# A retention and MLP kernel: seven products in the first MLP product from block 4 instead of 6, and a third of the v scalings on GpSimd

## The chip, the cores and the metric

The kernel runs on one core of a Trainium2 chip. TensorE (PE) multiplies matrices into PSUM, VectorE (DVE) and ScalarE (ACT) read PSUM and SBUF, GpSimd (POOL) works on SBUF and issues loads, SyncE (SP) issues transposing DMAs and stores. The metric is device time in microseconds, as the median of several runs; less is better.

## The reference

Inputs are q, k, v of shape (8, 8, 576, 64) and the weights `w_in` (512 x 2048) and `w_out` (2048 x 512), all float32. The output is (4608, 512) in float32.

```
scores = q @ k^T / sqrt(64)                       # per batch and head
D[i, j] = gamma_h ** (i - j) for i >= j, else 0   # gamma_h = 1 - 2 ** (-5 - h)
x = (scores * D) @ v, heads side by side          # 4608 tokens x 512
out = gelu_exact(x @ w_in) @ w_out
```

## The kernel before

Attention runs in 36 units of 128 tokens; four units make a block of 512 tokens, so there are nine blocks, 0 to 8. For a unit, TensorE forms the scores (L516, L525 or L535), VectorE applies the mask (`masked`, L558), TensorE multiplies with v (`inner`, L600) and adds what earlier tokens left in the state `u` (`cross`, L653), and VectorE moves the result into the tile `x` (`evacuate`, L672). The state itself is a product of k with v scaled by a decay (`state`, L619). That scaled v is the tile `vh`, made in `scaled_v`: eight small ScalarE instructions, one a head (L572), for the units in the set `BY_ACT`, else one VectorE instruction (L575).

Then each block passes an MLP. The first product, x times `w_in`, with gelu on the way out of PSUM into the tile `g`, has two forms. The plain one (`mlp1`, L701) takes 64 matmuls of 512 columns for a block. The other (`fast`, L966) is a Strassen-like scheme: in each of four groups it forms seven products of half-size blocks instead of eight, P1 to P7, with four matmuls of 256 columns each, 112 for a block. It needs sums of weights (`sum_in`, `sum_last`), sums of x (`sum_x`, L939), and copies and adds between PSUM banks, through a scratch tile `p`, between its steps (L981, L985 and L461). `FAST = 6` and `ALL_FAST = 6` say that blocks 6, 7 and 8 take it.

The second product, g times `w_out`, also has seven products (M1 to M7, `part`, L885) in all blocks but block 0 (`mlp2`, L746). Three sums of g for each group (`sum_g`, L782 to L786) and sums of w_out (`sum_w`) feed it; `after` moves and combines its results into the output tiles, which `store` sends out.

No scheduler of the compiler orders this. The kernel runs a planner while it is built: the table `T` holds a due time for each engine, `on` adds a cost to it, and the loop at the end picks what TensorE does next by ready times (`mlp_pick`, `part_ready`, `fast_ready`, `may_begin`). First and second products of neighbouring blocks are interleaved, and attention groups are put between them. `either` gives a copy to VectorE or ScalarE, whichever would end it first. The string `ORDER` lists the loads in the order in which GpSimd issues them, followed by tokens that shift single decisions: `a28` puts unit 28's v on ScalarE, `s4+1.5` delays scores, `p32+28` holds back a group of the first product, and so on. Each engine works through its own list in order; semaphores hold it back where data or a buffer is missing. Loads wait in GpSimd's queue like any other instruction. `warm` fills gaps before 16 us of the plan with matmuls on zeros.

Of the kernel before, what the change touches and what calls it, by code (L numbers as in the profile page):

```python
# [9 lines left out]
FP32 = mybir.dt.float32  # L10
BF16 = mybir.dt.bfloat16
# [6 lines left out]
def kernel(  # L18
# [52 lines left out]
    FAST, ALL_FAST = 6, 6  # L71
    N_LD = 5
    N_QKT = 4
# [6 lines left out]
    HOLD = 9  # L80

# [6 lines left out]
    g_pool = ctx.enter_context(tc.tile_pool(name="g", bufs=1))  # L88
# [53 lines left out]
    def constants():  # L142
# [7 lines left out]
        far_at = on("dve", 0.55, at)  # L150
        nc.vector.tensor_scalar(ident, val, 0.0, None, op0=ALU.is_equal)
        on("dve", 0.35)
# [6 lines left out]

    N_NEAR, NEAR = 5, (0, 2, 4, 6, 1, 3, 5, 7)  # L160
# [27 lines left out]
    def sum_w(i):  # L188
        w = w_out_sb[i]
        s = w_sum[i] = const.tile([128, 5, 256], BF16, name=f"w_sum{i}")  # L190
        b11, b12, b21, b22 = w[:, 0, 0:256], w[:, 0, 256:512], w[:, 1, 0:256], w[:, 1, 256:512]
        nc.vector.tensor_tensor(s[:, 0], b11, b22, op=ALU.add)
        nc.vector.tensor_tensor(s[:, 1], b12, b22, op=MINUS)
        nc.vector.tensor_tensor(s[:, 2], b21, b11, op=MINUS)
        nc.vector.tensor_tensor(s[:, 3:5], w[:, :, 0:256], w[:, :, 256:512], op=ALU.add)
        ws_at[i] = on("dve", 1.05, land_out[i]) + SEM

# [87 lines left out]
    def load(what, i):  # L285
# [8 lines left out]
        if what == "dq":  # L294
# [6 lines left out]
            dq_at[i] = on("pool", 1.2, dq_at[i - 1])  # L301
# [23 lines left out]
    for x, keys in enumerate(zip(*HW_FIRST)):  # L325
        for n, (what, i) in enumerate(keys):
# [3 lines left out]
    ORDER = ("wi1 k1 wi0 io q1 v0 q2 k2 v1 wi2 v2 k3 wi3 q3 v3 wi4 wi5 wi6 k4 q5 k5 q4 v5 wi7 wo1 wo0 k6 v4 dq2 "  # L330
# [7 lines left out]
             "b21+6.0").split()  # L338

    BY_ACT = {int(x[1:]) for x in ORDER if x[0] == "a"}  # L340
    S_LATE = {int(x[1:].split("+")[0]): float(x.split("+")[1]) for x in ORDER if x[0] == "s"}
    B_LATE = {int(x[1:].split("+")[0]): float(x.split("+")[1]) for x in ORDER if x[0] == "b"}
    DVE_LAG, P_WAIT, HURRY = ({int(x[1:].split("+")[0]): float(x.split("+")[1]) for x in ORDER if x[0] == kind} for kind in "zpu")
    ORDER = [x for x in ORDER if x[0] not in "abszpu"]
# [76 lines left out]
    DRAIN = 0.25  # L421
    SEM = 0.12
# [140 lines left out]
    def scaled_v(i):  # L563
# [5 lines left out]
        by_act = i in BY_ACT  # L569
        if by_act:  # L570
            for h in range(H):
                nc.scalar.activation(vh[:, h, :], loaded[i][1][:, h, :], AF.Copy, scale=dv[:, h, ci:ci + 1])  # L572
            st[i]["V"] = on("act", 2.0, at) + SEM
        else:
            nc.vector.tensor_tensor(vh, loaded[i][1], dv[:, :, ci:ci + 1].to_broadcast([128, H, D]), op=ALU.mult)  # L575
            st[i]["V"] = on("dve", 0.685, at) + SEM
# [109 lines left out]
    def g_of(t, mm):  # L686
        return g_tiles[t, mm // 2][:, mm % 2] if t else g_tiles[t, mm // 2][mm % 2]

    def g_done(t, j):
        if t > 0 and all((t, 4 * j + x, ts) in g_at for x in range(4) for ts in range(4)):  # L690
            at = max(g_at[t, 4 * j + x, ts] for x in range(4) for ts in range(4)) - SEM
            for x in range(3):
                queued.append((at, x, sum_g, (t, j, x)))
# [654 lines left out]
```

## Time and profile before

| | |
|---|---|
| median of 3 runs | 285.56 us (285.5 to 286.11) |
| span of the profiled execution | 283.7 us |
| TensorE busy | 278.0 us, 98% |
| VectorE busy | 199.7 us, 70% |
| ScalarE busy | 158.8 us, 56% |
| GpSimd busy | 114.0 us, 40% |
| mean granted TensorE clock | 0.998 |

The span reaches from the first to the last instruction of one execution; for that execution the page gives no time of its own beside it, so the median of the runs stands for it, 1.86 us more. Busy time of an engine counts its compute instructions; GpSimd's also counts the issuing of its loads. In the rows, "x60" is the number of instructions, then come busy time and the mean duration of one in ns, then the idle time before them with what ended it. In the timeline the first number is the start and the second the duration, in us.

### The profile page before, as it was taken

The page shows a single profiled execution, that of the slowest core. Times are in us where ns is not written, and L with a number is a line of the kernel's source. Part 1 is how long each engine was busy: PE and PEld are TensorE (multiplying, and loading weights), DVE is VectorE, ACT ScalarE, POOL GpSimd, SP SyncE. Part 2 cuts the span into 40 slices and gives each one's busy share as a digit, 9 for nine tenths or more (in the row PEclk, how much of TensorE's full clock was granted, in tenths as well). Part 3 has the DMA queues.
Part 4 walks back from the last instruction along what each step waited for, and adds up shares of the span by engine and source line. Part 5 has one row for each costly group of instructions (what it writes and reads, how often), then busy time and mean ns, then how long its engine had stood idle before and what let it go on. Part 6 is the DMA issues. An engine that isn't in the chain of part 4 may idle for free.

```text
span 283.7 us, 8075 instructions
## 1 busy us (share of the span) xinstructions
PE 278.0 (98%) x3361; PEld 207.6 (73%) x3361; DVE 199.7 (70%) x412; ACT 158.8 (56%) x362; POOL 114.0 (40%) x143
## 2 busy tenths in 40 slices
PE   8989999999999999999999999999999999999994
PEld 3577666688874588548855778558888888888894
DVE  5753483979865595898178867889669968966822
ACT  5676724755456635693298874564565374665320
POOL 8979987993364465625468552000000000000000
PEclk9999999999999999999999999999999999999999
DMA  9999999999999999999999999910003000400133
GB/s 150 165 182 173 188 180 163 146 142 147 172 161 195 190 147 128 156 229 149 135 197 203 147 137 150 222 21 2 0 2 128 23 2 0 151 0 2 74 114 111
DMA packets 152804, 35.39 MB, mean 125 GB/s; under 512 B 141120, under 2 KB 148928, under 8 KB 152768
## 3 DMA queue, kind: packets, MB, share of 16 engines
q0 software_dynamic: 116832, 18.10, 95.3%
q1 hardware_dynamic: 34528, 16.26, 32.9%
q10 hardware_dynamic: 1408, 0.52, 0.7%
q8 instruction: 26, 0.43, 0.7%
q14 instruction: 10, 0.08, 0.1%
HBM read 36.70 MB, written 9.44 MB: 163 GB/s over the span
## 4 chain that ended last, share of the span: by engine, by line
PE 92%; POOL 3%; DMA 3%; issue 0%; DVE 0%; POOLq 0%
PE m L885 35%; PE hT L701 29%; PE f L966 13%; PE oT L746 5%; PE o_ps L600 3%; PE sc L535 3%; DMA w_in<-in_moe_w_in_dram 3%; POOL qk L318 2%; PE o_ps L653 1%; PE u_ps L619 1%; PE qk_ps L482 1%; POOL v_ld L318 1%; POOL w_in L291 1%; PE sc L525 0%; PE o_ps L591 0%
## 5 line engine op out<-in xcount | busy, mean ns | idle before, releaser
L701 PE MATMUL hT<-xT,w_in 128*128 128x512 bf16 (+3 forms) x560 | 87.4, 312 | 0.8 <-DMA w_in<-in_moe_w_in_dram 0.8
L710 ACT ACTIVATE g<-hT 128x512 bf16<-128x512 f32 (+2 forms) x106 | 57.7, 556 | 36.9 <-PE hT L701 36.1
L701 PEld LDWEIGHTS <-w_in 128*128 128x128 bf16 x560 | 48.4, 98 | 33.8 <-DMA w_in<-in_moe_w_in_dram 1.0
L885 PEld LDWEIGHTS <-gs 128*128 128x128 bf16 x656 | 62.2, 98 | 7.7
L885 PE MATMUL m<-w_sum,gs 128*128 128x256 bf16 (+1 forms) x400 | 47.7, 268 | 0.0
L318 POOL DMA_DIRECT2D v_ld<-in_v_dram x40 | 34.0, 854 | 19.3 <-DMA qk_ld<-in_k_dram 8.8
L318 POOL DMA_DIRECT2D qk_ld<-in_k_dram x36 | 30.4, 851 | 21.7 <-DMA qk_ld<-in_q_dram 19.1
L558 DVE TENSOR_TENSOR ret<-sc,msk 128x512 bf16<-128x512 f32 x48 | 30.2, 683 | 12.2 <-PE sc L535 12.2
L318 POOL DMA_DIRECT2D qk_ld<-in_q_dram x36 | 30.4, 851 | 16.9 <-DMA qkT<-qk_ld 6.5
L885 PE MATMUL m<-w_out,gs 128*128 128x256 bf16 x256 | 32.5, 273 | 0.0
L885 PE MATMUL m<-w_sum,g 128*128 128x256 bf16 x256 | 30.9, 273 | 0.0
L572 ACT ACTIVATE vh<-v_ld,dv 128x64 bf16<-128x64 bf16 x120 | 30.0, 339 | 0.0
L782 DVE TENSOR_TENSOR gs<-g 128x1024 bf16<-128x1024 bf16 x32 | 21.8, 686 | 9.0 <-ACT g L710 8.2
L885 PEld LDWEIGHTS <-g 128*128 128x128 bf16 x256 | 24.9, 98 | 3.9
L991 ACT ACTIVATE g<-f 128x512 bf16<-128x512 f32 x36 | 20.2, 590 | 8.9 <-PE f L966 7.5
L786 DVE TENSOR_TENSOR gs<-g 128x1024 bf16<-128x1024 bf16 x32 | 21.6, 684 | 0.0
L672 DVE TENSOR_TENSOR xT<-o_ps,dqT 128x512 bf16<-128x512 f32 (+1 forms) x32 | 18.4, 617 | 4.5 <-PE o_ps L653 4.4
L966 PEld LDWEIGHTS <-w_in 128*128 128x128 bf16 x192 | 18.8, 98 | 2.2
L461 ACT CAST u_sb<-u_ps 128x512 bf16<-128x512 f32 x15 | 8.7, 587 | 16.0 <-PE u_ps L619 16.0
L461 ACT COPY o<-m 128x512 f32<-128x512 f32 x14 | 8.2, 587 | 15.7 <-PE m L885 15.7
L987 ACT ACTIVATE g<-p 128x512 bf16<-128x512 f32 x12 | 7.6, 630 | 14.1 <-DVE p L985 14.1
L966 PEld LDWEIGHTS <-wi 128*128 128x128 bf16 x144 | 14.0, 98 | 1.6
(96 smaller groups left out, 337.6 us busy)
## 6 DMA issues: line engine op xcount, KB each, us to landing
out_dram<-o SPq DMA_DIRECT2D x27, 256.0 KB, 6.3
v_ld<-in_v_dram POOLq DMA_DIRECT2D x32, 128.0 KB, 9.1
qk_ld<-in_k_dram POOLq DMA_DIRECT2D x28, 128.0 KB, 10.7
qk_ld<-in_q_dram POOLq DMA_DIRECT2D x28, 128.0 KB, 8.6
w_in<-in_moe_w_in_dram POOLq DMA_DIRECT2D x8, 256.0 KB, 7.3
w_out<-in_moe_w_out_dram POOLq DMA_DIRECT2D x8, 256.0 KB, 8.0
out_dram<-o SPq DMA_DIRECT2D x14, 128.0 KB, 2.1
qk_ld<-in_q_dram POOLq DMA_DIRECT2D x8, 64.0 KB, 11.4
```

Of the source, the lines that this page charges most:

```text
L318: nc.gpsimd.dma_start(dst, src[2 * bp + jj, :, ci * C:ci * C + n, :].rearrange("h s d -> s h d"))
L461: nc.scalar.copy(dst, src)
L558: nc.vector.tensor_tensor(r, t, by, op=ALU.mult)
L572: nc.scalar.activation(vh[:, h, :], loaded[i][1][:, h, :], AF.Copy, scale=dv[:, h, ci:ci + 1])
L672: nc.vector.tensor_tensor(x_of(i)[:, :, n * x:n * x + n], o, dqT[:, :, ci * C:ci * C + n], op=ALU.mult)
L701: nc.tensor.matmul(hT[:, m, :], lhsT=w[:, cc, o:o + 128], rhs=x_tiles[t][:, cc, lo:hi], start=(cc == 0), stop=(cc == N_DM - 1))
L710: nc.scalar.activation(g_of(t, m0 // 2)[:, m0 % 2:m0 % 2 + n, lo:hi], hT, AF.Gelu)
L782: nc.vector.tensor_tensor(s.rearrange("p m a b -> p m (a b)"), g[:, :, 0, :], g[:, :, 1, :], op=ALU.add)
L786: nc.vector.tensor_tensor(s, g[:, :, :, LEFT], g[:, :, :, RIGHT], op=MINUS)
L885: nc.tensor.matmul(m[:, 0 if apart else ts, :], lhsT=a, rhs=w[:, c0:c1], start=p in begins and mm == 0 and ts == 0, stop=mm == N_DF // 2 - ...
L966: nc.tensor.matmul(m[:, y, :], lhsT=a[:, c], rhs=d[:, c], start=p in (P1, P7) and y == 0 and c == 0, stop=c == 1, skip_group_check=True)
L991: nc.scalar.activation(g[:, :, rows, cols], m, AF.Gelu)
```

## The change

The first product takes its seven-product form from block 4 on, so in blocks 4 to 8. The tile `g` of a block is cut in two halves that turn through three buffers, and the scratch tile `p` goes: its place is the part of `g` that is written last. Thirteen of the 36 v scalings move to GpSimd (tokens `g23` and the like in `ORDER`), four stay on ScalarE (fifteen before), nineteen on VectorE (21 before). The seven products of the second product are replaced by another set of seven, Q1 to Q7, which takes four sums of half the tile in place of three, each over two groups at once, except in the last block; its results are added in the output tile. The planner's costs are changed in places, it reckons with GpSimd and VectorE hindering each other, and the string `ORDER` is another one, with other loads from `wi4` on and other shifts. The diff, cut to its core:

```diff
-    FAST, ALL_FAST = 6, 6
+    FAST, ALL_FAST = 4, 4
     N_LD = 5
+    N_G = 3
...
-    g_pool = ctx.enter_context(tc.tile_pool(name="g", bufs=1))
+    g_pool = ctx.enter_context(tc.tile_pool(name="g", bufs=N_G))
...
-    def on(engine, dur, ready=0.0):
+    def on(engine, dur, ready=0.0, pair=False):
         lap = 0.075 if engine == "dve" and dur > 0.2 else 0.0
-        T[engine] = max(T[engine], ready) + dur - lap
+        start = max(T[engine], ready)
+        if pair:
+            for a, b in port[-2:]:
+                if a < start + dur and start < b:
+                    start = max(start, b - 0.1)
+            pairs_read.append((start, start + dur))
+        elif engine == "pool" and dur > 0.6:
+            for a, b in pairs_read[-4:]:
+                if a < start + dur and start < b:
+                    T["dve"] = max(T["dve"], min(start + dur + 0.5, T["dve"] + 1.5))
+            port.append((start, start + dur))
+        T[engine] = start + dur - lap
...
-    ORDER = ("wi1 k1 wi0 io q1 v0 q2 k2 v1 wi2 v2 k3 wi3 q3 v3 wi4 wi5 wi6 k4 q5 k5 q4 v5 wi7 wo1 wo0 k6 v4 dq2 "
+    ORDER = ("wi1 k1 wi0 io q1 v0 q2 k2 v1 wi2 v2 k3 wi3 q3 v3 wi4 q4 wi5 wi6 wo1 k4 q5 k5 dq2 v4 wo0 wi7 q6 v5 "
...
-        if by_act:
+        if i in BY_POOL:
+            nc.gpsimd.tensor_tensor(vh, loaded[i][1], dv[:, :, ci:ci + 1].to_broadcast([128, H, D]), op=ALU.mult)
+            st[i]["V"] = on("pool", POOL_V, at) + SEM
+        elif i in BY_ACT:
...
+        g_tiles[t, j // 2] = g_pool.tile([128, 4, 2, TOK], BF16, tag="g", name="g")
...
-    bank_of = {M3: "X", M4: "Y", M5: "X", M1: "Z", M2: "Y", M6: "V", M7: "Z"}
-    begins = {M3, M4}
-    behind = {M5: M3, M1: M4, M2: M4, M6: M1, M7: M1}
+    bank_of = {Q1: "X", Q6: "X", Q5: "X", Q3: "X", Q7: "V", Q4: "V", Q2: "Y"}
+    begins = {Q1, Q7}
+    behind = {Q6: Q1, Q2: Q1, Q4: Q7, Q5: "C21", Q3: "C22"}
...
-        if n == 0:
-            nc.vector.tensor_tensor(s.rearrange("p m a b -> p m (a b)"), g[:, :, 0, :], g[:, :, 1, :], op=ALU.add)
-        elif n == 1:
-            nc.vector.tensor_tensor(s[:, :, 0], g[:, :, 0, LEFT], g[:, :, 1, RIGHT], op=ALU.add)
-        else:
-            nc.vector.tensor_tensor(s, g[:, :, :, LEFT], g[:, :, :, RIGHT], op=MINUS)
+        o, a, b, op = {S1: (s1, a21, a22, ALU.add), S2: (s2, s1, a11, MINUS), S3: (s3, a11, a21, MINUS), S4: (s4, a12, s2, MINUS)}[n]
+        nc.vector.tensor_tensor(o, a, b, op=op)
...
+        nc.vector.tensor_tensor(hi[:, xs, d + c0:d + c1], m, hi[:, xs, d + c0:d + c1], op=ALU.add)
...
-            if not p7_tiles:
-                p7_tiles.append(ld_pool.tile([128, 2, 2, 256], FP32, tag="qk", bufs=N_LD, name="p7"))
-            f_bank[key, "p7"] = p7_tiles[0][:, j % 2]
+            f_bank[key, "p7"] = g.rearrange("p m a b -> p m (a b)")[:, :, 256:768].bitcast(FP32)
...
+    SEQ = (Q1, Q7, Q6, Q4, Q5, Q3)
+    FILL = ((Q5, (0, 1, 2, 3)),)
...
-            runs.append([("3", t, p, k) for p in range(7) for k in range(4)])
+            order = [(p, k) for p in SEQ for k in range(4) if p != Q2]
+            for at, ks in FILL if t < N_BLK - 1 else ((Q5, range(4)),):
+                n = order.index((at, 0)) if at is not None else len(order)
+                order[n:n] = [(Q2, k) for k in ks]
+            runs.append([("3", t, p, k) for p, k in order])
```

More of the change, by code (lines that the diff above doesn't have):

```diff
@@ new lines, in add_out @@
+    def add_out(t, n, what, done, ready):
+        hi = o_tiles[t, 1]
+        last = t == N_BLK - 1
+        b, m = held_bank[t, "X", n]
+        xs, c0, c1 = pieces(t)[n]
+        d = 256 * (what == "C22")
+        nc.vector.tensor_tensor(hi[:, xs, d + c0:d + c1], m, hi[:, xs, d + c0:d + c1], op=ALU.add)
+        seen(t, what, n, on("dve", 0.15 + 0.00104 * (xs.stop - xs.start) * (c1 - c0), max(done, ready)))
+        if last and n != 1:
+            x = xs.start
+            store(t, 2 + x, hi[:, x, d:d + 256], d, d + 256, *((nc.scalar, nc.scalar) if n else ()))
+        elif what == "C22" and not last:
+            for x in range(2):
+                store(t, 2 + x, hi[:, x, :])
```

308 lines of the change are left out of this document (177 added, 131 removed), and 15 rows, old and new, of the table ORDER.

## The prediction

> **What bounds the kernel now.** I read the page's head first, then the waits of TensorE, then its timeline.
>
> ```profile
> span 283.7 us, 8075 instructions
> PE 278.0 (98%) x3361; PEld 207.6 (73%) x3361; DVE 199.7 (70%) x412; ACT 158.8 (56%) x362; POOL 114.0 (40%) x143
> PE 92%; POOL 3%; DMA 3%; issue 0%; DVE 0%; POOLq 0%
> PE warm L1187 <- DVE zeros L118: 1.2, 1, 1.2
> PE hT L701 <- DMA w_in<-in_moe_w_in_dram: 0.8, 1, 0.8
> ```
>
> TensorE is busy for 98% of the span, and the chain that ended last runs through it for 92%. The two waits are all that the view of waits lists for its matmuls: 1.2 us before the first warm-up matmul and 0.8 us for a weight load. No wait for VectorE or ScalarE appears after that. So the span is the number of matmuls times their spacing, and a change is worth what it does to that product, as long as no new wait appears.
>
> The profiled span is 283.7 us and the median of the runs 285.56 us; the 1.86 us between them lie outside the span, and I keep them. The sum below is a difference, added to 285.56 us.
>
> **The price of one matmul.** A matmul's own duration (379 ns for 512 columns) includes the pipeline, so I take spacings from starts in the timeline of TensorE.
>
> ```profile
> 68.05 3.66 PE L885 MATMUL m<-w_sum,g 128*128 128x256 bf16 x32
> 71.54 1.91 PE L885 MATMUL m<-w_out,gs 128*128 128x256 bf16 x16
> 73.38 0.32 PE L591 MATMUL o_ps<-ret,vh 64*64 64x64 bf16 x16
> 73.53 0.30 PE L653 MATMUL o_ps<-qkT,u_sb 64*64 64x64 bf16 x16
> 73.76 0.61 PE L885 MATMUL m<-w_sum,gs 128*128 128x256 bf16 x4
> 80.29 0.64 PE L600 MATMUL o_ps<-ret,vh 128*64 128x128 bf16 x16
> ...
> 81.90 1.49 PE L885 MATMUL m<-w_sum,gs 128*128 128x256 bf16 x12
> 83.22 13.11 PE L701 MATMUL hT<-xT,w_in 128*128 128x512 bf16 x60
> 96.27 0.64 PE L600 MATMUL o_ps<-ret,vh 128*64 128x128 bf16 x16
> 217.31 0.60 PE L966 MATMUL f<-xT,wi 128*128 128x256 bf16 x4
> 217.84 0.64 PE L600 MATMUL o_ps<-ret,vh 128*64 128x128 bf16 x16
> ```
>
> With 256 columns: 71.54 - 68.05 = 3.49 us for 32, 0.109 us each. Four take 0.436 us, but 217.84 - 217.31 is 0.53: going from whole-array matmuls to the tiled ones of the attention costs 0.09 us. Sixteen 64x64 matmuls take 0.15 us (73.38 to 73.53) when the same tiling follows, and 0.23 us (73.53 to 73.76) when whole-array ones follow: the way back costs 0.08 us. With 512 columns: 96.27 - 83.22 = 13.05, less the 0.09 of the switch, by 60: 0.216 us. One group of the attention, 80 tiled matmuls, takes 81.90 - 80.29 = 1.6 us with its way back.
>
> **The change, part by part: TensorE.** Blocks 4 and 5 leave the plain first product. Each loses 64 matmuls of 512 columns (L701: 264 before, 136 in the built program after, 128 fewer for two blocks) and gets 112 of 256 columns.
>
> ```profile
> L701 PE MATMUL hT<-xT,w_in 128*128 128x512 bf16 x264 | 59.0, 379 | 0.0
> L966 PE MATMUL f<-xs,w_in 128*128 128x256 bf16 x96 | 14.4, 273 | 0.0
> L885 PE MATMUL m<-w_sum,gs 128*128 128x256 bf16 x368 | 46.7, 273 | 0.0
> ```
>
> That is -128 x 0.216 = -27.6 us and +224 x 0.109 = +24.4 us: -3.2 us. The second product keeps its seven products in other sums: 880 matmuls of 256 and 32 of 128 columns become 864 and 64, the same columns, and 16 more starts, some 0.1 us with the eight 384-column matmuls of block 0 that are cut into 24 of 128. Counted in the built programs, TensorE goes into tiled stretches 37 times where it went 31 times, and switches between tilings 13 times where it did 16: 6 x (0.09 + 0.08) - 3 x 0.09 = +0.75 us. Two more warm-up matmuls of 512 columns stand before the attention: +0.43 us if they fill no wait, nothing if they do; I take the whole. TensorE: -3.2 + 0.1 + 0.75 + 0.43 = -1.9 us.
>
> **VectorE and ScalarE.** Durations, one row for each kind:
>
> ```profile
> L558 DVE TENSOR_TENSOR ret<-sc,msk 128x512 bf16<-128x512 f32 x48 | 30.2, 683 | 12.2 <-PE sc L535 12.2
> L572 ACT ACTIVATE vh<-v_ld,dv 128x64 bf16<-128x64 bf16 x120 | 30.0, 339 | 0.0
> L782 DVE TENSOR_TENSOR gs<-g 128x1024 bf16<-128x1024 bf16 x32 | 21.8, 686 | 9.0 <-ACT g L710 8.2 <-PE m L885 0.7
> L786 DVE TENSOR_TENSOR gs<-g 128x1024 bf16<-128x1024 bf16 x32 | 21.6, 684 | 0.0
> L672 DVE TENSOR_TENSOR xT<-o_ps,dqT 128x512 bf16<-128x512 f32 x24 | 15.4, 683 | 1.3 <-PE o_ps L653 1.2
> L784 DVE TENSOR_TENSOR gs<-g 128x512 bf16<-128x512 bf16 x32 | 13.4, 419 | 0.1
> L985 DVE TENSOR_TENSOR p<-p,f 128x512 f32<-128x512 f32 x12 | 8.2, 686 | 6.0 <-PE f L966 6.0
> L461 ACT COPY p<-f 128x512 f32<-128x512 f32 x10 | 5.9, 588 | 2.1 <-PE f L966 2.1
> L939 DVE TENSOR_TENSOR xs<-xT 128x512 bf16<-128x512 bf16 x6 | 2.3, 417 | 0.0
> 49.89 1.28 DVE L558 TENSOR_TENSOR ret<-sc,msk 128x512 bf16<-128x512 f32 x2
> ```
>
> The sums for the second product go from 56.8 us (the three gs rows) to 56 of 0.686 and 16 of 0.419, 45.1 us. Sixteen more adds for the seven products at L985's 0.686 are +11 us; eight more xs are +3.4; output adds and seeds that become plain copies, split between the two engines, come to little. VectorE stays near 200 us in all. ScalarE loses 88 of the 120 v multiplications (30.0/120 = 0.25 us each, 22 us) and gains some 15 copies at 0.588: 12 to 13 us less in all.
>
> What matters is the stage. In the built program's order, between the 14th group of scores and the last, where blocks 4 to 7 have both their products beside the attention, VectorE has 96 instructions: 26 masks, 11 xT, 16 gs, 12 xs, 20 adds of the first product and copies, 6 output steps, 3 v, 2 states. By the rows that is 62 us; back to back they overlap (two masks in 1.28, not 1.37), some 0.07 each, so 56 us are occupied. TensorE has 467 matmuls of 256 columns there and 479 tiled ones, six groups of 80: 467 x 0.109 + 6 x 1.6 = 61 us. So VectorE would be 92% occupied for 61 us, with 5 us free. The nearest rows:
>
> ```profile
> core 0: us, PE busy (x) PEld busy (x) DVE busy (x) ACT busy (x) POOL busy (x), PEclk, DMA share, GB/s
> 160.00:180.00 20.00, 20.00 (x264) 14.87 (x261) 14.68 (x30) 12.99 (x40) 6.40 (x9) 1.00 1.99 148
> 180.00:200.00 20.00, 20.00 (x275) 14.00 (x275) 18.12 (x36) 10.10 (x18) 0.00 (x0) 1.00 0.31 65
> 200.00:220.00 20.00, 20.00 (x222) 17.73 (x220) 14.69 (x27) 11.97 (x22) 0.00 (x0) 1.00 0.13 49
> ```
>
> In 180 to 200 us VectorE was 91% busy and TensorE still had no wait, at the full granted clock (1.00). That carries the forecast, but only over 20 us. I put the waits that come of it between 0 and 6.7 us (the upper end is worked out below) and take 0.5, near the row's zero.
>
> **GpSimd.** Thirteen of the 36 v multiplications go there, 88 instructions of ScalarE (11 units) and two of VectorE less. None was there before; the nearest rows are its own multiplication of 512 float elements and VectorE's for v:
>
> ```profile
> L575 DVE TENSOR_TENSOR vh<-v_ld,dv 128x512 bf16<-128x512 bf16 x21 | 14.3, 700 | 0.0
> L299 POOL TENSOR_TENSOR dqT<-dqT,step 128x512 f32<-128x512 f32 x2 | 2.1, 1058 | 0.0
> 51.09 1.05 DVE L575 TENSOR_TENSOR vh<-v_ld,dv 128x512 bf16<-128x512 bf16 x1
> 50.93 0.65 POOL L299 TENSOR_TENSOR dqT<-dqT,step 128x256 f32<-128x256 f32 x1
> ```
>
> I take 1.06 us, between 0.7 and 1.5: 14 us on an engine with nothing left to do after 180 us (0.00 in its column above). It issues in order, so the load issues behind a multiplication wait until that v has landed. Seven of the thirteen stand behind the last load and hold up nothing; the other six could each hold the loads behind them for 1 us, which a load ahead of its use hides; the price without that cover is 6 us, and I take none.
>
> The last two rows show the danger. A v multiplication on VectorE that began 0.16 us after one on GpSimd took 1.05 us where its mean is 0.70: 0.35 us lost. The gs, xs, wi and v instructions read two SBUF tiles as that one did; masks and xT read PSUM. At 0.35 us the eleven multiplications of units 20 to 35 take 3.9 us from VectorE, inside the 5 us that it has free in that stretch, so I count no wait. If each takes its whole 1.06 us, it is 11.7 us and no longer inside: that is the second rival.
>
> The Trainium skill, page "SBUF — State Buffer", section "Who interferes with whom", has a rule that speaks against this change: a VectorE instruction with two inputs in SBUF and a GpSimd instruction that reads SBUF exclude each other, and the one that comes later waits until the other has ended. The trace agrees, in its one case. By the row as it stands the sum is the forecast's; by the rule, with a VectorE instruction arriving at the start of every one, it is the second rival's.
>
> **The end.** The last block ends as before on a 128-column piece, an instruction of some 0.3 us and a store. I take 0, between -0.3 and +0.5.
>
> Sum: -1.9 (TensorE) + 0.5 (waits) = -1.4 us, so 285.56 - 1.4 = 284.2 us.
>
> **The rivals.** First, the gain is used up by waits of the first product's own chain. In one group of it four steps follow each other (L966 four matmuls, 0.436 us), with a copy or add of 0.59 to 0.69 us and 0.3 us assumed for handing over between them: 4 x 0.44 + 3 x 1.0 = 4.7 us, hidden while two groups alternate (2 x 7 x 0.436 = 6.1 us). It has 1.4 us to spare. Before, at most 24 such matmuls stand together with no second-product work between; in the built program 56, a whole pair of groups, stand together once, behind scores whose four masks (2.4 us) come first on VectorE. Blocks 4 to 7 have eight such pairs; 0.24 us of waiting at each gives back 1.9 us, which is 285.6 us. Against it: the 5 us that VectorE has free.
>
> Second, slower: VectorE becomes the bound between the 14th group of scores and the end of the attention, because GpSimd's multiplications block it. 56 + 11.7 = 67.7 us against TensorE's 61: 6.7 us of waits, 285.56 - 1.9 + 6.7 = 290.4 us. It decides from about 0.45 us lost per multiplication on, where eleven of them use up the 5 us; halfway, at 0.75 us, it costs 3.3 us, 287.0 us. For it speaks the row of 0.35 us; against it, that under half of VectorE's instructions there read two SBUF tiles. The loads' 6 us would lead to the same side.
>
> Third, a larger gain: the warm-ups fill a wait (0.43) and the 0.8 us wait for w_in goes, with no waits in the stretch: -1.9 - 0.43 - 0.8 = -3.1, 282.5 us. For it speaks only that the order of loads differs.
>
> **How the numbers follow.** I give the forecast 0.57, the first rival 0.19, the second 0.19, the third 0.05. Within 0.2%, which is about what a measurement of this kernel can tell from no change, means 285.0 to 286.1 us. The forecast's own range, 283.6 to 284.9, lies below that, the third rival too: faster 0.62. The first rival spreads over both sides of no change, most of it within: same 0.14, and 0.05 go with the second rival to slower, 0.24. The range that holds 8 in 10 leaves out the third rival and the worse half of the second: 283.2 to 287.2 us.
>
> **What would show it.** Right: 136 matmuls of 512 columns in the plain first product and 560 in the seven-product one, at unchanged spacing; no entry for VectorE in TensorE's waits over 0.5 us; VectorE 85 to 95% busy from 150 to 215 us; GpSimd's multiplications near 1.06 us. Wrong: a gap of TensorE before f or m matmuls that ends on VectorE, gs or xs instructions over 1 us beside GpSimd's, loads that land late, or spacings other than 0.109 and 0.216.

## The result, and the profile after

| | median | runs |
|---|---|---|
| before | 285.56 us | 9, 285.46 to 286.35 |
| changed | 287.11 us | 9, 285.94 to 289.13 |
| ratio | 1.0063 | 95% interval 1.0039 to 1.0088 |

The change makes the kernel slower by 0.6%, where the prediction had 284.2 us. The time lies in the predicted range, but on the wrong side of no change. A ratio compares the undisturbed runs of both kernels, so it need not be the quotient of the medians. The profiled execution of the changed kernel took 289.13 us, the slowest of its nine, with a span of 287.4 us; beside it I use another profiled execution of the same kernel (changed_again below, 286.68 us).

The head of the changed kernel's page and the view of TensorE's waits. A row of that view names who waits for whom, then the us in total, the number of times and the longest:

```profile
span 287.4 us, 8281 instructions
PE 277.6 (97%) x3491; PEld 217.4 (76%) x3491; DVE 209.2 (73%) x415; ACT 145.2 (51%) x287; POOL 128.0 (45%) x156
PE 86%; DVE 4%; POOL 4%; DMA 3%; issue 1%; ACT 1%; POOLq 0%; DVEq 0%
...
PE qk_ps L500 <- DMA qk<-in_q_dram: 2.8, 3, 1.6
PE warm L1268 <- DVE zeros L134: 1.2, 1, 1.2
PE m L944 <- DVE gs L821: 0.9, 1, 0.9
PE sc L553 <- DVE xT L692: 0.8, 1, 0.8
PE f L1028 <- DVE g L1045: 0.4, 1, 0.4
PE f L1028 <- DVE f L1041: 0.2, 1, 0.2
```

TensorE's share of the chain falls from 92% to 86%. Before, the only wait for VectorE was the one for the zeros of the warm-ups; now four more are listed. The first of the listed waits is for loads at the start and differs from run to run (0.6 us in changed_again); the four for VectorE come later. Groups of instructions by shape, then VectorE's busy time in the stretch that the prediction looked at:

```profile
L738 PE MATMUL hT<-xT,w_in 128*128 128x512 bf16 x136 | 30.7, 379 | 0.0
L1045 DVE TENSOR_TENSOR g<-g,f 128x512 f32<-128x512 f32 x20 | 13.7, 685 | 10.0 <-PE f L1028 7.1 <-ACT g L1051 3.0
L588 POOL TENSOR_TENSOR vh<-v_ld,dv 128x512 bf16<-128x512 bf16 x13 | 13.7, 1073 | 19.9 <-PE u_ps L639 11.7 <-issue 8.1
```

```profile
core 0: us, PE busy (x) PEld busy (x) DVE busy (x) ACT busy (x) POOL busy (x), PEclk, DMA share, GB/s
150.00:170.00 20.00, 20.00 (x324) 17.16 (x323) 18.14 (x32) 10.52 (x23) 14.96 (x18) 1.00 1.92 184
170.00:190.00 20.00, 19.63 (x248) 16.93 (x247) 17.15 (x29) 11.13 (x21) 7.30 (x9) 1.00 1.14 124
190.00:210.00 20.00, 19.10 (x317) 16.07 (x312) 16.27 (x27) 9.52 (x19) 3.12 (x3) 1.00 0.22 54
```

Counts and GpSimd's 1.073 us are as forecast, and so is VectorE's load (91%, 86%, 81%), but for the last row, which lies below the 85 to 95%; the granted clock is 1.00. What is new is that TensorE idles: 0.37 and 0.90 us in the last two stretches. The timeline of the changed kernel shows one of these places (start, duration, then in brackets the idle time before the instruction):

```profile
190.45 0.69 DVE L474 CAST u_sb<-u_ps 128x512 bf16<-128x512 f32 x1 [0.94 <-PE u_ps L639]
190.46 2.07 POOL L588 TENSOR_TENSOR vh<-v_ld,dv 128x512 bf16<-128x512 bf16 x2 [11.73 <-PE u_ps L639]
...
191.66 2.02 DVE L821 TENSOR_TENSOR gs<-g 128x1024 bf16<-128x1024 bf16 x2
...
193.13 1.59 PE L944 MATMUL m<-w_sum,gs 128*128 128x256 bf16 x13 [0.90 <-DVE gs L821]
```

Two scalings on GpSimd run from 190.46 to 192.53. Two sums of g, which take 1.28 us elsewhere, take 2.02: the first alone is held until 193.08 us (1.42 us), and the second product's matmuls start right behind it. The two scalings had been free to start only when TensorE's `u_ps` (L639) released a buffer, so they fall where the sums stand.

**The account.** I took the starts of consecutive matmuls from the traces and added up what exceeds their usual spacing by more than 0.13 us, apart from some places of 0.22 us where a record is missing. The column "first to last such matmul" is the time from the first second-product matmul of block 1 (at 68.05 us in the kernel before) to the last matmul of the program, and "rest" is that time without the waits after 30 us. The sums of waits are good to some 0.2 us, since they hang on what is taken for the usual spacing.

| profiled run | waits before 30 us | waits after | first to last such matmul | rest |
|---|---|---|---|---|
| before | 0.9 | 0 | 211.7 | 211.7 |
| changed | 3.3 | 3.7 | 213.6 | 209.9 |
| changed_again | 1.1 | 3.0 | 212.8 | 209.8 |

TensorE's own work became 1.9 us shorter there, and 3.0 to 3.7 us of waits took its place. The experiments ask where these waits come from. None of them touches the planner or TensorE's order of matmuls; only what is issued for single steps differs.

### The profile page after: what moved, and what is told of

Same layout as the page of the kernel before. It is cut to its first block, busy times and chain, and to the rows that moved or that the text cites. A ratio compares the mean times of both kernels' runs of the same rounds, so it can differ in the third digit from the quotient of the medians.

```text
span 287.4 us, 8281 instructions
## 1 busy us (share of the span) xinstructions
PE 277.6 (97%) x3491; PEld 217.4 (76%) x3491; DVE 209.2 (73%) x415; ACT 145.2 (51%) x287; POOL 128.0 (45%) x156
## 4 chain that ended last, share of the span: by engine, by line
PE 86%; DVE 4%; POOL 4%; DMA 3%; issue 1%; ACT 1%; POOLq 0%; DVEq 0%
PE m L944 31%; PE f L1028 21%; PE hT L738 18%; PE oT L778 5%; DMA qk<-in_q_dram 3%; PE o_ps L620 3%; PE sc L553 3%; POOL qk L336 2%; DVE gs L821 1%; PE u_ps L639 1%; PE o_ps L673 1%; PE qk_ps L500 1%; POOL w_in L309 1%; POOL v_ld L336 1%; DVE xT L692 1%
## 5 line engine op out<-in xcount | busy, mean ns | idle before, releaser
L738 PE MATMUL hT<-xT,w_in 128*128 128x128 bf16 (+3 forms) x448 | 59.4, 288 | 0.0
L742 ACT ACTIVATE g<-hT 128x512 bf16<-128x512 f32 (+2 forms) x75 | 39.4, 535 | 32.0 <-PE hT L738 31.4
L944 PEld LDWEIGHTS <-gs 128*128 128x128 bf16 x536 | 49.5, 98 | 8.0 <-DVE gs L821 1.3
L944 PE MATMUL m<-w_sum,gs 128*128 128x256 bf16 (+1 forms) x400 | 49.6, 269 | 1.0 <-DVE gs L821 0.9
L1051 ACT ACTIVATE g<-f 128x512 bf16<-128x512 f32 x60 | 33.8, 596 | 25.5 <-DVE f L1041 22.8
L944 PEld LDWEIGHTS <-g 128*128 128x128 bf16 x392 | 37.3, 98 | 4.7
L944 PE MATMUL m<-w_out,g 128*128 128x256 bf16 (+1 forms) x264 | 33.1, 270 | 0.0
L821 DVE TENSOR_TENSOR gs<-g 128x1024 bf16<-128x1024 bf16 (+1 forms) x36 | 21.7, 644 | 5.1 <-ACT g L742 5.1
L1028 PE MATMUL f<-xs,wi 128*128 128x256 bf16 x160 | 24.0, 273 | 0.2 <-DVE f L1041 0.2
L1028 PE MATMUL f<-xs,w_in 128*128 128x256 bf16 x160 | 23.9, 273 | 0.0
L1028 PE MATMUL f<-xT,w_in 128*128 128x256 bf16 x160 | 23.8, 273 | 0.0
L588 POOL TENSOR_TENSOR vh<-v_ld,dv 128x512 bf16<-128x512 bf16 x13 | 13.7, 1073 | 19.9 <-PE u_ps L639 11.7
```

What stands on the lines that cost most here:

```text
L588: nc.gpsimd.tensor_tensor(vh, loaded[i][1], dv[:, :, ci:ci + 1].to_broadcast([128, H, D]), op=ALU.mult)
L738: nc.tensor.matmul(hT[:, m, :], lhsT=w[:, cc, o:o + 128], rhs=x_tiles[t][:, cc, lo:hi], start=(cc == 0), stop=(cc == N_DM - 1))
L742: nc.scalar.activation(g_of(t, m0 // 2)[:, m0 % 2:m0 % 2 + n, lo:hi], hT, AF.Gelu)
L821: nc.vector.tensor_tensor(o, a, b, op=op)
L944: nc.tensor.matmul(m[:, 0 if apart else ts, :], lhsT=a, rhs=w[:, c0:c1], start=p in begins and mm == 0 and (ts == 0 or apart), stop=mm == ...
L1028: nc.tensor.matmul(m[:, y, :], lhsT=a[:, c], rhs=d[:, c], start=p in (P1, P7) and y == 0 and c == 0, stop=c == 1, skip_group_check=True)
```

## The experiments

The theory was the prediction's second rival: GpSimd's multiplications hold VectorE's instructions. Rivals were the first product's own chain, VectorE's plain load, and the loads.

### GpSimd's multiplications taken away, doubled, and nothing changed

The thirteen scalings go to ScalarE, in the same place of the program:

```diff
-            nc.gpsimd.tensor_tensor(vh, loaded[i][1], dv[:, :, ci:ci + 1].to_broadcast([128, H, D]), op=ALU.mult)
+            for h in range(H):
+                nc.scalar.activation(vh[:, h, :], loaded[i][1][:, h, :], AF.Copy, scale=dv[:, h, ci:ci + 1])
```

> The changed kernel, TensorE's order untouched, with the 13 v scalings that it gives to GpSimd made by ScalarE (eight small instructions each) in the same places. Theory A, GpSimd's scalings block VectorE's two-input instructions and those make TensorE wait: the waits of TensorE near 73-77 and 188-193 us (2.7 us in the profiled run) go, and the time falls by 2 to 3 us to about 284.5, unless ScalarE's 26 us more of work make waits of their own. Theory B, VectorE is overfull from block 4 on whatever GpSimd does: these waits stay, 287 us. Theory C, the loss is in the first 21 us, where TensorE waits for loads of q: nothing changes by more than 0.5 us.

Measured: 295.22 us (6 runs, 294.29 to 296.4), ratio 1.0327 [1.0296, 1.0358], far on the wrong side. TensorE's waits:

```profile
PE f L1029 <- ACT g L1052: 2.8, 1, 2.8
PE f L1029 <- ACT f L479: 2.2, 2, 1.4
```

The waits for the sums are gone from the list, but the first product now waits for ScalarE, which has eight small instructions more for each unit, 2 us together. So this run moves the load and doesn't remove it, and says little on the theory.

Each scaling on GpSimd done twice, the second time into a spare tile:

```diff
+            nc.gpsimd.tensor_tensor(spare, loaded[i][1], dv[:, :, ci:ci + 1].to_broadcast([128, H, D]), op=ALU.mult)
```

> The changed kernel with every one of the 13 GpSimd scalings followed by a second, equal one into a spare tile that nobody reads. Theory A: twice the time in which GpSimd holds VectorE off, 2 to 4 us slower than the changed kernel (about 290). Theory B and theory C: within 0.5 us of the changed kernel, since GpSimd has idle time.

Measured: 291.12 us (4 runs, 290.46 to 291.4), ratio 1.0181 [1.0155, 1.0207]. In its timeline a sum of g is held through both:

```profile
73.26 2.64 DVE L823 TENSOR_TENSOR gs<-g,gs 128x1024 bf16<-128x1024 bf16 x1
...
73.27 1.07 POOL L589 TENSOR_TENSOR vh<-v_ld,dv 128x512 bf16<-128x512 bf16 x1
74.29 1.06 POOL L590 TENSOR_TENSOR spare<-v_ld,dv 128x512 bf16<-128x512 bf16 x1
```

Not every pair holds a sum so long: from 158.03 us on the two multiplications take 1.54 and 1.49 us and the two sums beside them 1.54 us each, so there the engines take turns, and both lose. Eight VectorE instructions beside the scalings are longer than the median of their kind, by 8.8 us together, against four and 3.8 us in changed_again; the waits after 30 us rise from 3.0 to 6.6 us. More GpSimd, more waits.

The changed kernel and the kernel before once more:

> The changed kernel once more, for a second profile. Theory A: TensorE again waits behind VectorE's gs near 76 and 193 us. Theory C: the waits for loads of q before 21 us (3.3 us in the first profile) are there again. If the first profile was only an unlucky one, they are under 1.5 us and the time is about 286.

> The kernel before once more, for a second profile: 285.5 to 286.3 us. Theory C needs that its loads of q land before TensorE asks for them, with no wait over 0.3 us ahead of 17 us, as in the first profile; if it waits there as the changed kernel does, the start is a matter of the run and not of the change.

Measured: 287.72 us (10 runs, 286.28 to 291.35), ratio 1.0049 [1.0024, 1.0073], and 285.46 us. The four instructions that lost 3.8 us are sums of g at 73.53 (1.70 us instead of 0.69), 156.19 (1.15) and 189.18 us (1.42), and a weight sum at 119.36 us, whose timeline reads:

```profile
119.36 1.88 DVE L992 TENSOR_TENSOR wi<-w_in,wi 128x256 bf16<-128x256 bf16 x1
...
119.99 1.09 POOL L588 TENSOR_TENSOR vh<-v_ld,dv 128x512 bf16<-128x512 bf16 x1
```

It takes 0.29 us elsewhere. Its recorded start lies 0.6 us ahead of GpSimd's scaling, and it is held all the same, until 0.16 us after the scaling's end. Between the two starts GpSimd was issuing a load (119.30 to 120.00 us); in no_read below, the same sum of weights beside such an issue takes its usual 0.29 us, so the issue alone doesn't hold it. This one costs TensorE nothing: no wait follows it. Nor does the hold at 73.53 us in this execution; in the first profile the sum of g ahead of that one was held 1.2 us at 74.01, and TensorE lost some 1.3 us behind it, at 76.3 and 76.6. The hold at 189.18 us stands behind the 1.06 us at 190.7, of which 0.32 remain in no_read, where nothing is held.

The hold at 156.19 us (0.46 us lost) costs TensorE 0.29 us, but five microseconds later. From 155 to 162 us VectorE is busy without a gap (7.00 of 7 us), so it hands the delay on to the x tile that the scores at 161.6 us need. Other profiles bear this out: a sum there that loses 0.77 us is followed by a wait of 0.56 us (moved_aside below), one that loses 0.86 by 0.75 us in two parts (own_scratch), and in no_read, where none is held, there is no wait.

### Reading or occupied time

GpSimd fills the tile with zeros in place of scaling, once and twice:

```diff
-            nc.gpsimd.tensor_tensor(vh, loaded[i][1], dv[:, :, ci:ci + 1].to_broadcast([128, H, D]), op=ALU.mult)
+            nc.gpsimd.memset(vh, 0.0)
+            nc.gpsimd.memset(vh, 0.0)      # in no_read_same_time only
```

> The changed kernel, TensorE's order untouched, with the 13 scalings on GpSimd replaced by filling the tile with zeros, so that GpSimd reads nothing there (this leaves out the product of v with its decay for 13 of 36 units). Theory A, it is GpSimd's reading of SBUF that holds VectorE's two-input instructions off: no gs or wi instruction over 1 us, TensorE's wait for gs near 190 us falls from 1.06 to under 0.4 us, the time falls by 1 to 2 us to 285.3 to 286.2. Theory B, an overfull VectorE: wait and time stay (286.7 to 287.7). Neither takes away the waits before 21 us nor those of the first product's own chain (1.3 us in the second profile).

> Each of the thirteen v scalings on GpSimd is replaced by two fillings with zeros, one after the other (2 x 0.556 us = 1.11 us by the row of the single filling, against 1.075 us for the multiplication): GpSimd is occupied as long as in the changed kernel, writes the same tile twice and reads nothing of SBUF. The run leaves out v times the decay in 13 units. If it is the reading that holds VectorE: as with the single filling, 285.5 us (285.2 to 285.9), no sum of g over 0.75 us beside GpSimd, and no wait of 1 us before the second product near 190 us. If it is the time that GpSimd takes, or the moment at which the scaled tile is ready: 287.1 to 287.7 us, as the changed kernel.

Measured: 285.49 us (12 runs, 285.1 to 286.58), ratio 0.9996 [0.9983, 1.0008], and 285.43 us (12 runs, 284.9 to 286.55), ratio 0.9988 [0.9971, 1.0004]. The two fillings of no_read_same_time, where 1073 ns stood for one multiplication:

```profile
L588 POOL MEMSET vh<- 128x512 bf16 x13 | 7.0, 542 | 18.3 <-PE u_ps L640 18.3
L589 POOL MEMSET vh<- 128x512 bf16 x13 | 6.8, 525 | 0.7
```

With GpSimd occupied for the same time (1.1 us a unit) and writing the same tile, but reading nothing, the loss is gone, and no sum of g is longer than usual. So it is the reading that costs, 1.6 to 2.2 us by the two medians of the changed kernel. TensorE's waits of no_read:

```profile
PE f L1028 <- DVE g L1045: 0.4, 1, 0.4
...
PE f L1028 <- DVE f L1041: 0.2, 1, 0.2
PE m L944 <- DVE gs L821: 0.2, 1, 0.2
```

But without the reading the kernel is only level with before. By the account 1.8 us of waits stay after 30 us: 0.53 us at 185.8, 0.32 at 189.2, 0.35 at 222.7 and smaller ones. That is about as much as TensorE's work became shorter.

### The same reading where VectorE has room

In the kernel before, the ten scalings that ScalarE made for units from 17 on go to GpSimd (the expectation says nine from 18 on; the edit and the trace have ten):

```diff
+        if by_act and i > 16:
+            nc.gpsimd.tensor_tensor(vh, loaded[i][1], dv[:, :, ci:ci + 1].to_broadcast([128, H, D]), op=ALU.mult)
```

> The kernel before, TensorE's order untouched, with the nine v scalings that it gives to ScalarE from unit 18 on made by GpSimd, all else as before: one part of the change alone. Theory A: VectorE's two-input instructions beside them take 1 us and more here too, but VectorE has more idle time, so the waits of TensorE come to 0.5 to 2 us (286 to 287.5 us). Theory B: no waits, 285.5 us or a little less. If GpSimd's loads are held up behind the scalings, TensorE waits for scores or v instead, from 150 us on.

Measured: 285.95 us (12 runs, 284.95 to 287.46), ratio 0.9997 [0.9968, 1.0026]. VectorE is held here too, for 2.7 us over four instructions, and GpSimd is slowed with it (two scalings take 2.60 us instead of 2.13):

```profile
146.91 1.05 DVE L785 TENSOR_TENSOR gs<-g 128x1024 bf16<-128x1024 bf16 x1 [1.06 <-ACT g L713]
147.46 2.60 POOL L571 TENSOR_TENSOR vh<-v_ld,dv 128x512 bf16<-128x512 bf16 x2
147.88 1.27 DVE L787 TENSOR_TENSOR gs<-g 128x512 bf16<-128x512 bf16 x1
149.08 1.54 DVE L789 TENSOR_TENSOR gs<-g 128x1024 bf16<-128x1024 bf16 x1
```

TensorE has no wait after 30 us, so the 0.5 to 2 us of waits that the expectation's theory A had did not come. A hold alone costs nothing: it must reach an instruction that TensorE needs before VectorE has caught up.

In the changed kernel, units after 28 are scaled in place, so that GpSimd need not wait for a buffer and can be through before 187 us:

```diff
-        vh = vh_pool.tile([128, H, D], BF16, tag="vh", name="vh")
+        vh = loaded[i][1] if i in BY_POOL and i > 28 else vh_pool.tile([128, H, D], BF16, tag="vh", name="vh")
```

> The changed kernel with the GpSimd scalings of units 29, 30, 31, 33, 34 and 35 written over the loaded v instead of into one of the six vh buffers, so that GpSimd need not wait for a free buffer until 188 us and is through with them by about 181 us. All is computed. Theory A: the wait near 190 us falls to under 0.4 us, since no GpSimd instruction runs beside gs there; another may appear between 174 and 181 us; 0.5 to 1 us faster than the changed kernel. Theory B: the wait near 190 us stays at 1 us and the time too.

Measured: 288.77 us (12 runs, 285.95 to 293.48), ratio 1.0041 [1.0011, 1.0071]. The executions spread widely: six lie from 285.95 to 287.48 us with a mean granted clock of 0.998 or more, six from 290.06 us up with 0.992 to 0.994. The profiled one is the slowest of them (293.48 us), so what follows explains that one and not the median:

```profile
181.39 5.10 POOL L588 TENSOR_TENSOR v_ld<-v_ld,dv 128x512 bf16<-128x512 bf16 x5
...
182.19 4.86 DVE L595 TENSOR_TENSOR vh<-v_ld,dv 128x512 bf16<-128x512 bf16 x1
```

Five scalings came one behind the other, and a VectorE instruction of 0.68 us got through only after the last, 4.86 us in all. TensorE waited 4.0 us for what stood behind it. From 187.81 to 191.22 us the granted clock is 0.5, and a matmul of 256 columns takes 0.213 us instead of 0.109, which costs some 1.5 us more. The wait before the second product at which the edit aimed did fall, to 0.30 us. The low mean clock of the five others suggests that they too had such a wait; why six escape it isn't shown, since only one was profiled.

### VectorE's load

The sums of g become copies of their first input:

```diff
-        nc.vector.tensor_tensor(o, a, b, op=op)
+        nc.vector.tensor_copy(o, a)
```

> The changed kernel, TensorE's order and GpSimd's 13 scalings untouched, with each of VectorE's sums for the second product (gs) replaced by a copy of its first input (this leaves out the adding). If a copy is faster than the 0.69 us of a sum, VectorE has some 15 us less to do from block 1 on. Theory A+B joined, GpSimd costs time only because VectorE is 92% full between 150 and 215 us: the waits near 187, 190 and 222 us go, time 284.0 to 284.8 us, which is the gain that the count of matmuls promised. Theory A alone, in which it is the hold itself: the wait near 190 us stays near 1 us and the time over 285.5 us.

Measured: 285.24 us (12 runs, 284.56 to 291.04), ratio 0.9975 [0.9953, 0.9997]. A copy takes 0.436 us instead of 0.69. The waits near 222 and 250 us, where a first-product add stands behind sums in VectorE's list, are gone; that near 189.5 us stays, at 0.8 us, and the two copies ahead of it, beside GpSimd's reading, take 1.50 us:

```profile
188.31 1.50 DVE L821 COPY gs<-g 128x1024 bf16<-128x1024 bf16 x2
```

A lighter VectorE helps, but the hold remains. The copies are not free of GpSimd either: at 64 to 66 us, where GpSimd only issues loads, two of them take 0.90 and 0.84 us.

Then work goes from VectorE to ScalarE: the copies out of PSUM between 124 and 262 us of the plan, in the second run without those of the first product's chain:

```diff
-            if by is None:
+            if by is None and 124.0 < T["pe"] < 262.0:                      # copies_on_scalar
+            if by is None and 124.0 < T["pe"] < 262.0 and not chain[0]:     # some_copies_on_scalar
+                nc.scalar.copy(dst, src)
```

> The changed kernel, TensorE's order untouched, with the 24 copies out of PSUM that the plan gives to VectorE between the start of block 4 and the last block made by ScalarE in the same places (17 us less on VectorE, 14 us more on ScalarE, which is 51% busy). All is computed. Theory A+B joined: shorter waits for VectorE near 187, 190 and 222 us, but copies in the first product's chain now queue behind gelus: between 1.5 us faster and 1 us slower than the changed kernel. Theory A alone: no change from 286.7 to 287.7.

> As the run with all copies on ScalarE, but only the nine of output, x and state tiles, none of the first product's chain: 6 us less on VectorE. Theory A+B joined: the wait near 190 us shorter by some 0.7 us (the output copy near 186 us and the copies of u and x near 188 us, all ahead of gs, leave VectorE), 0.5 to 1 us faster than the changed kernel. Theory A alone: no change.

Measured: 288.56 us (6 runs), ratio 1.0094 [1.0069, 1.012], and 287.61 us (12 runs), ratio 1.0059 [1.0036, 1.0082]. No gain; the wait of 1.06 us before the second product near 191 us stands in both (the view of waits lists `m L944 <- DVE gs L821` in each with the same 0.9 us). For this wait it isn't the other work on VectorE that counts, but what runs beside the sums. On VectorE's load as a whole these two runs say less, since ScalarE's copies bring waits of their own (0.3 us of attention for a copy on ScalarE is listed in both).

### The place of the reading, and the rest

Units 33 and 34, the two beside the sums near 189 us, are scaled on ScalarE, the other eleven on GpSimd as before:

```diff
+            if i in (33, 34):
+                for h in range(H):
+                    nc.scalar.activation(vh[:, h, :], loaded[i][1][:, h, :], AF.Copy, scale=dv[:, h, ci:ci + 1])
```

> Only the scalings of units 33 and 34, the two beside which the sums of g were held near 189 us, go from GpSimd to ScalarE (16 instructions of some 0.25 us, 4 us); the other eleven stay. If that place is where the loss is made: the wait of the second product for the sums near 190 us (1.06 us) and the one behind it go, 286.2 to 286.9 us. If what ScalarE gets is late for its copies, as when it took all thirteen: waits of the first product for ScalarE of 1 us or more near 190 us and 287.5 us or above.

Measured: 291.41 us (5 runs, 291.18 to 291.95), ratio 1.0202 [1.0183, 1.022]. The wait near 190.6 us fell from 1.06 to 0.30 us, as the theory has it (another hold, of a sum at 71.14 us, stands before a wait of 1.2 us at 72.8 in this execution). But ScalarE works in order, and the two scalings, which GpSimd ran at 188 us, far ahead of their place in the program, stand late in its list:

```profile
209.84 0.60 ACT L1055 ACTIVATE g<-f 128x512 bf16<-128x512 f32 x1
210.33 3.90 ACT L590 ACTIVATE vh<-v_ld,dv 128x64 bf16<-128x64 bf16 x16
214.14 0.58 ACT L1055 ACTIVATE g<-f 128x512 bf16<-128x512 f32 x1
```

A gelu stands 3.9 us behind them, and TensorE waits 3.0 us at 214.8. From 215.76 to 219.17 us the granted clock is then 0.5, which costs 1.7 us more. It is the mishap of v_on_scalar, at a place where it can be read.

Then the reading is moved and not removed. GpSimd first fills the tile with zeros, which holds nobody, and scales later:

```diff
+            for _ in range({11: 2, 33: 12}.get(i, 0)):
+                nc.gpsimd.memset(vh, 0.0)
             nc.gpsimd.tensor_tensor(vh, loaded[i][1], dv[:, :, ci:ci + 1].to_broadcast([128, H, D]), op=ALU.mult)
```

> As the changed kernel, but GpSimd fills the scaled tile with zeros before it scales, twice before unit 11 and twelve times before unit 33 (0.55 us each, writing without reading): the scalings of units 33 and 34 move from 188.0 to some 194.6 us, where VectorE applies masks, and that of unit 11 from 73.6 to 74.7 us, behind the sums of g. If the moment of the reading is what costs: TensorE's wait of 1.06 us near 190 us falls to some 0.3 us, that near 73 us goes, 0.8 to 1.5 us less than the changed kernel, 285.8 to 286.6 us. If the amount of reading counts, wherever it stands: 287.1 to 287.7 us.

Measured: 286.44 us (12 runs, 285.77 to 288.97), ratio 1.0037 [1.0011, 1.0063]. The timeline shows what was wanted:

```profile
187.85 6.93 POOL L589 MEMSET vh<- 128x512 bf16 x12 [11.36 <-PE u_ps L641]
194.87 2.07 POOL L590 TENSOR_TENSOR vh<-v_ld,dv 128x512 bf16<-128x512 bf16 x2
...
189.07 1.28 DVE L823 TENSOR_TENSOR gs<-g 128x1024 bf16<-128x1024 bf16 x2
...
193.19 2.48 DVE L576 TENSOR_TENSOR ret<-sc,msk 128x512 bf16<-128x512 f32 x4
```

The two sums take 1.28 us again, and the four masks beside the moved scalings take their usual 2.48: a mask has one input in SBUF and one in PSUM. The wait near 190 us falls to 0.32 us. The one of 0.2 us near 71 us stays, though I had expected it to go; it lies ahead of the moved scaling. By the ratios alone the run can't be told from the changed kernel (its interval overlaps both of that kernel's); it is the trace that shows the effect.

Next, the scratch of the first product gets a tile of its own, outside of g, in bf16; the zeros of the warm-ups shrink to make room:

```diff
-            f_bank[key, "p7"] = g.rearrange("p m a b -> p m (a b)")[:, :, 256:768].bitcast(FP32)
+            f_bank[key, "p7"] = p7_own[:, j % 2]
```

> As the changed kernel, but the scratch of the seven-product form no longer lies inside the tile g: it has a tile of its own, in bf16 (the memory does not suffice for float32, so the running sum of two of the seven products is rounded to bf16 once more), and the zeros tile of the warm-ups is half as large and read twice. If the add waits for ScalarE's gelu only because both write into g: the idle time of 0.49 us before the add near 185 us goes, and with it TensorE's wait of 0.53 us; 0.5 us less than the changed kernel, 286.6 to 287.1 us. If the add would be late anyway: the wait stays, 287.1 to 287.7 us.

Measured: 286.68 us (12 runs, 285.84 to 289.3), ratio 1.0037 [1.0011, 1.0063]. The timelines of VectorE around that add, first of no_read, where the scratch is in g, then of own_scratch:

```profile
183.90 0.69 DVE L821 TENSOR_TENSOR gs<-g,gs 128x1024 bf16<-128x1024 bf16 x1
185.08 0.69 DVE L1045 TENSOR_TENSOR g<-g,f 128x512 f32<-128x512 f32 x1 [0.49 <-ACT g L1051]
```

```profile
185.11 0.69 DVE L822 TENSOR_TENSOR gs<-g,gs 128x1024 bf16<-128x1024 bf16 x1
185.72 0.68 DVE L1046 TENSOR_TENSOR p_own<-p_own,f 128x512 bf16<-128x512 bf16 x1
```

The add no longer waits for ScalarE, and TensorE's wait there falls from 0.53 to 0.18 us; here too the ratio alone doesn't tell the run from the changed kernel. The gelu that it waited for writes other columns of g, so the order was kept for a place in the tile and not for data. Both edits together:

> Both edits of own_scratch and moved_aside together. If the two causes are separate and both real: the two gains add, 1.3 to 2.0 us less than the changed kernel, 285.2 to 286.1 us, level with the kernel before or a little faster. If one hides behind the other: no better than moved_aside, 285.8 to 286.6 us.

Measured: 286.26 us (12 runs, 285.15 to 290.86), ratio 1.0016 [0.9991, 1.0041]. That is 0.16 us above what was expected, and level with the kernel before: the interval does not tell them apart. Its median lies below the changed kernel's, and not below before's. Last, all known causes are taken away: no reading by GpSimd, copies for the sums, and the scratch in its own tile.

> All the causes taken away together: GpSimd fills with zeros where it scaled (v times the decay is left out in 13 units), the sums of g are copies of 436 instead of 690 ns (their adding is left out), and the scratch has a tile of its own. If blocking, the chain and the sums are what uses up the gain: TensorE's waits fall to about 1 us, start included, and the time comes near TensorE's own sum, 283.7 to 284.6 us. If something else holds 1 us or more: 284.9 us or above, with waits or spacings that say what.

Measured: 283.98 us (6 runs, 283.25 to 284.67), ratio 0.9932 [0.991, 0.9955]. The whole list of TensorE's waits:

```profile
PE qk_ps L501 <- DMA qk<-in_q_dram: 1.3, 2, 1.1
PE warm L1269 <- DVE zeros L135: 1.1, 1, 1.1
```

It leaves out work that the result needs, so it isn't a version. It closes the account:

| profiled run | waits after 30 us | first to last such matmul | rest |
|---|---|---|---|
| changed_again | 3.0 | 212.8 | 209.8 |
| own_scratch | 2.8 | 212.7 | 209.9 |
| moved_aside | 2.6 | 212.4 | 209.8 |
| no_read | 1.8 | 211.6 | 209.8 |
| aside_and_own | 1.3 | 211.3 | 210.0 |
| no_read_light_own | 0.1 | 209.9 | 209.8 |

The rest is 209.8 to 210.0 us in every one; the waits alone differ.

## Why the prediction was wrong, point by point

- **TensorE's sum, -1.9 us: right in kind.** 136 and 560 matmuls stand where they were forecast, at the spacings of 0.216 and 0.109 us. From the first second-product matmul on, the rest fell by 211.7 - 209.8 = 1.9 us. Without the warm-ups the sum had -2.35 us, nearly all of it there; where the other 0.4 us went stays open. Ahead of that point the sum had +0.43 us of warm-ups. Whether they came isn't shown: the changed profiles reach the point 0 to 0.75 us later than before (68.05 us in moved_aside, 68.28 in no_read, 68.80 in no_read_light_own; the first profile 2.2 us), and their waits for loads at the start differ by as much. With its later waits away, no_read_light_own ends at 283.98 us, 1.5 us below the 285.53 us of before beside it; the interval of its ratio allows 1.3 to 2.6 us, so the -1.9 is not refuted.
- **Waits, +0.5 us: the step that failed.** I took the wait of one row of the kernel before, near zero, for the whole stretch. The trace has 3.0 us in changed_again and 3.7 in the first profile, where before had none. In changed_again -1.9 + 3.0 makes the stretch 1.1 us longer (212.8 against 211.7 us) and, with start and end, the span 1.2 us longer (284.9 against 283.7). The measured loss is 287.11 - 285.56 = 1.55 us, by the ratio 1.1 to 2.5. That execution is a quick one (286.68 us, where the median of its ten is 287.72), so the waits of a typical one are known only roughly.
- **The price of a hit, 0.35 us: mis-sized.** I took it from one instruction that began 0.16 us after a GpSimd multiplication of 0.65 us, and spread it over eleven. The measured hits are fewer (four in changed_again) but cost 0.5 to 1.6 us each, 3.8 us together: the scaling lasts 1.07 us, two stand in a row, and an instruction that began a little earlier is held too. That the total agrees with the 3.9 us of the prediction is luck.
- **The sum of the hits against VectorE's free time: the wrong comparison.** 3.8 us lost would have fitted into the 5 us free, as the 2.7 us of before_v_gpsimd cost nothing. But the hits at 189 us, and in the first profile that at 74 us, fall on instructions with matmuls close behind them, and that at 156 us on a VectorE that has no free time for the next 5 us: free time averaged over 61 us is of no use there. By the waits after 30 us the reading costs 3.0 - 1.8 = 1.2 us in changed_again (0.74 at 190.7 us, 0.29 at 161.6 us and some 0.2 at 171.8 us, whose cause is open) and 1.9 in the first profile; by the medians 1.6 to 2.2. The second rival's mechanism is shown by no_read, no_read_same_time and moved_aside. Its condition, VectorE full over the whole stretch, came true only in places, and its 290.4 us not at all.
- **The first rival, 0.24 us at each of eight pairs, 285.6 us.** no_read has 285.49 us with 1.8 us of waits. So its amount was right, by luck, but not its shape: there is no 0.24 us at each pair, but 0.53 us where the add waits for a gelu, 0.32 us of the second product behind the sums, which isn't this chain at all, and 0.35 us where an add stands behind sums and evacuations in VectorE's list.
- **The scratch inside g: counted at nothing, and not priced.** I had not named what the new place of the scratch makes wait. It is 0.35 us by own_scratch's trace. Both rivals came true together; I had given each 0.19 and no chance to their sum.
- **The Trainium skill,** page "SBUF — State Buffer", section "Who interferes with whom": that only a GpSimd instruction which reads SBUF excludes a two-input one of VectorE agrees with no_read and moved_aside (fillings hold no sum). I had set the rule beside the one row of 0.35 us and followed the row; the rule's price, a wait until the other ends, was the better one. By the recorded starts the trace doesn't follow the rule throughout: at 119.36 us the instruction that began first was held, and in before_v_gpsimd the scalings were slowed as well (1.41 and 1.22 us).
- **GpSimd 1.06 us, the loads, the end:** 1.073 us measured. No wait for a load is listed after 30 us in the changed kernel, so the loads' price of 6 us did not appear. From the last matmul's start to the end of the span it is 3.5 to 3.9 us in the profiles of the kernel before and of before_v_gpsimd, and 3.6 us in the two of the changed kernel: no difference to be told.

## What to carry to other kernels

Work moved to an idle engine is free only if it doesn't hold a neighbour at a moment at which a critical step stands behind it, or at which the neighbour has no free time before the next such step: look at what the new instruction reads, and what the other engine has in hand then, before averaging a loss over free time. An engine that runs ahead of the plan does its work at other times than the plan has it; moving it in time (here by 7 us, beside work out of PSUM) can be worth more than giving it to another engine, as two_on_scalar shows. Where a scratch is folded into a tile to save memory, list who else writes that tile, for each can become a wait (0.35 us here).

## What the runs showed of the hardware

- A VectorE instruction with two SBUF inputs is held by a GpSimd multiplication whose recorded start lies up to 0.6 us after its own (119.36 against 119.99 us in changed_again): 1.88 us instead of 0.29.
- Multiplications on GpSimd without a gap can let a waiting VectorE instruction through only behind the last: 2.64 us beside two (gpsimd_twice, 73.26 us), 4.86 us beside five (v_in_place). They don't always: at 158.03 us of gpsimd_twice sums and multiplications take turns at 1.5 us each.
- GpSimd fillings (0.52 to 0.65 us for 512 bf16 elements in no_read and no_read_same_time) hold no sums of g.
- VectorE's copies from SBUF to SBUF, with one input, are held too: 1.50 us for two beside GpSimd's reading (light_sums), 0.76 without it (no_read_light_own).
- At the end of a TensorE wait, or 1 us behind it, of 3.0 us (v_on_scalar to 218.39 us, two_on_scalar to 214.76 us) or 4 us (v_in_place to 188.30 us) the granted clock is 0.5 for 3.41 us, once each, and a 256-column matmul takes 0.213 us instead of 0.109. Behind the waits of up to 1.8 us in these traces it stays at 1.00.
